# Gated linear attention and two MLPs on one core: three weight buffers, later-placed loads, and first-chunk f, k, q loaded in 768-byte rows

## The chip, the cores and the metric

The kernel runs on one core of a Trainium2 chip. The core has five engines with queues of their own: TensorE (PE in the profile; its weight loads are shown apart as PEld), VectorE (DVE), ScalarE (ACT), GpSimd (POOL) and SyncE (SP), which here issues the DMAs. Each engine takes its instructions strictly in the order of its queue and waits at the head of it for what the instruction needs. The metric is the device time of one execution in microseconds; lower is better, and the median of three runs counts.

## What is computed

Four batches, eight heads, 768 tokens and head size 48. A gated linear attention walks over the tokens of each head, and its output (3072 tokens of 384 numbers) passes through two MLPs.

```python
# q, k, v, f_logit: (4, 8, 768, 48); w_in: (384, 2048), w_out: (2048, 384)
f = 1.0 / (1.0 + np.exp(-f_logit))
state = np.zeros((B, H, D, D))
for t in range(S):
    state = f[:, :, t, :, None] * state + np.einsum('bhd,bhe->bhde', k[:, :, t], v[:, :, t])
    y[:, :, t] = np.einsum('bhd,bhde->bhe', q[:, :, t], state)
...
h = x @ w_in                                        # first MLP
x = (np.maximum(h, 0) + alpha * np.minimum(h, 0)) @ w_out
h = x @ w2_in                                       # second MLP
out = (h - np.tanh(h)) @ w2_out
```

The weights come as 64-bit floats and are turned into pairs of 32-bit parts (a rounded part and its remainder) on the chip; a product of the MLPs is made of three matmuls of such parts.

## The kernel before

**Attention.** The tokens are cut into 6 chunks of 128. A step i is one batch of one chunk (i = 4 * chunk + batch), so there are 24 steps. A step has seven stages. Stage f turns f so that channels lie on partitions (`turned`, four transposes on PE), takes exp and adds one on ACT into the one `gate` tile, and makes the running product `up` and the backward one `down` with two scans on DVE, the second of which reads `gate` too. Stage k turns k and q and multiplies them by `up` and `down` on DVE (kd, qd). Stage s0 makes the scores on PE, which ACT copies to `a` and POOL masks in the first two chunks; s1 turns kd back for the state. Stage y0 multiplies qd by the state of earlier chunks (`blocks`), y1 the masked scores by v, and the sum is split on ACT and DVE into the two parts of x. Stage m renews the state on DVE and copies it into `blocks` on ACT. From the second chunk on, some rows of x have to move to other partitions (`x_spread`, six DMAs of 32 KB for each pair of steps).

**MLPs.** A slot is one 128-wide piece of the 2048 hidden columns for one chunk's 512 tokens: nine matmuls into h, the nonlinearity and a split into gh and gl on ACT and DVE, and two slots later nine matmuls into the accumulators. The first eight pieces of chunk 0 come first (slots 0 to 7), then all sixteen of chunk 1, which need all four steps 4 to 7.

**Weights.** Each MLP's weights are 16 halves of 768 KB. `load_w` brings a half into a staging tile `raw` (pool `stg`), and `convert` decodes it: |high word| on ACT (mag), then four integer operations on DVE (L50, L52, L55, L58), a rounding copy on ACT and a subtraction on DVE (L200). `stg` has two buffers, and the load of half n+2 stands right behind the decode of half n.

**What sets the order.** The first four steps follow the hand-written list `PROLOGUE`; everything later has a due time in slots, put into `work` and sorted; Tile's scheduler then lays the instructions of that program out on each engine's queue. All DMAs go through SP's queue, at most eight under way at once: a further one waits for the completion of the one eight places ahead. The f, k and q tiles (three of each) are zero-padded from 48 to 64 columns by POOL, only in the padding (L120).

Of the kernel before, what the change touches and what calls it, by code (L numbers as in the profile page):

```python
# [25 lines left out]
SEG = C + 1  # L26
NV = 3
X3W = 2
LAG = 2
# [34 lines left out]
def tile_main(tc, q, k, v, f_logit, w1_in, w1_out, alpha, w2_in, w2_out, out, flag):  # L64
    nc = tc.nc
    with ExitStack() as ctx:
# [4 lines left out]
        stg = ctx.enter_context(tc.tile_pool(name="stg", bufs=2))  # L71
# [29 lines left out]
        for b in range(B):  # L101
            state.append(const.tile([128, NP, D], F32, name=f"state{b}"))
            t = const.tile([128, NP, 2, HW], F32, name=f"blocks{b}")
            nc.gpsimd.memset(t, 0.0)
            blocks.append(t)
# [10 lines left out]
        for nm, idle in (("f", 30.0), ("k", 0.0), ("q", 0.0)):  # L116
# [18 lines left out]
        def load_step(i):  # L135
            c, b = divmod(i, B)
            t0 = c * C
            s = {}
            for nm, a in (("f", f_logit), ("k", k), ("q", q), ("v", v)):
                if nm == "v" and c == 0:  # L140
                    s["v"], s["v3"] = first_v[b % NV]
                    nc.sync.dma_start(out=s["v"][:, :, 0:D], in_=v[b, 0:6, t0:t0 + C, :].rearrange("h t d -> t h d"))
                    for h in range(2):
                        nc.sync.dma_start(
                            out=s["v3"][:, h, :, D:64], in_=v[b, 6 + h, t0:t0 + C, :].rearrange("t (r d) -> t r d", r=3)
                        )
                    continue
                if nm == "v":
                    t = s[nm] = ld.tile([128, H, D], F32, tag=nm, name=nm, bufs=NV)
                else:  # L150
                    s[nm] = padded[nm][i % NV]
                    t = s[nm][:, :, 0:D]
                nc.sync.dma_start(out=t, in_=a[b, :, t0:t0 + C, :].rearrange("h t d -> t h d"))  # L153
            steps[i] = s

# [53 lines left out]
        def turned(a, palloc, name):  # L209

            t = palloc([128, NP, C], name)
            for p in range(NP):
                nc.tensor.transpose(t[:, p], a[:, 2 * p:2 * p + 2, :].rearrange("t h d -> t (h d)"), ident)  # L213
            return t

        def attn_f(i, palloc):
            s = steps[i]
            gv = spread(gate[:, 0:NP * SEG])
            ft = turned(s["f"], palloc, "ft")
            nc.scalar.activation(out=gv, in_=ft, func=ACTF.Exp, scale=-1.0)  # L220
# [21 lines left out]
        def attn_k(i, palloc):  # L242
            s = steps[i]
            kt, qt = turned(s["k"], palloc, "kt"), turned(s["q"], palloc, "qt")
            kd = at.tile([128, NP, C], F32, tag="kd", name="kd")
            nc.vector.tensor_tensor(out=kd, in0=kt, in1=spread(s["up"]), op=ALU.mult)
            qd = at.tile([128, NP, C], F32, tag="qd", name="qd")
            nc.vector.tensor_tensor(out=qd, in0=qt, in1=spread(s["down"][:, 1:NP * SEG + 1]), op=ALU.mult)
            s.update(kd=kd, qd=qd, a=at.tile([128, 2, NP, C], F32, tag="a", name="a"))

        def attn_s(i, half, palloc):
            s = steps[i]
            if half:
# [6 lines left out]
                return  # L260

# [20 lines left out]
        def attn_y(i, half, palloc):  # L282
            c, b = divmod(i, B)
            s = steps[i]
            if half == 0:
                y = s["y"] = palloc([128, NP, C], "y")
                if c:
                    for p in range(NP):
                        nc.tensor.matmul(  # L289
                            out=y[:, p], lhsT=blocks[b][:, p].rearrange("p h d -> p (h d)"), rhs=s["qd"][:, p],  # L290
# [47 lines left out]
        def attn_m(i, palloc):  # L338
# [18 lines left out]
            for h in range(2):  # L357
                r = slice(HW * h, HW * h + HW)
                nc.scalar.copy(out=blocks[b][r, :, h, 0:D], in_=st[r])
# [131 lines left out]
        def stage(st, i, palloc=narrow):  # L491
# [22 lines left out]
        load_step(0)  # L514
        nc.sync.dma_start(out=alpha_raw, in_=alpha.rearrange("(c p) -> c p", p=128))
        load_step(1)
        load_w(0, *halves[0])
        load_step(2)
        load_w(0, *halves[1])

        for ev in PROLOGUE:
            if ev[0] == "c":
                convert(0, ev[1])
            elif ev[0] == "l":
                load_step(ev[1])
            else:
# [11 lines left out]
        for i in range(B, NC * B):  # L538
# [6 lines left out]
            for st, t in order:  # L545
                put(t0 + t, stage, st, i)
        first = sum(ev[0] == "c" for ev in PROLOGUE)
        for n in range(first, 2 * NG):
            put((n - first) * 1.0 if n < NG else 7.5 + 1.5 * (n - NG), convert, 0, n)
# [4 lines left out]
        for n in range(2):  # L554
            put(last + 1.5, load_w, 1, *halves[n])
        for n, (g, half) in enumerate(halves):
            put(max(last + 6 + 1.5 * n, last + 2 * g + 2 * half + 2.2), convert, 1, n)
# [170 lines left out]
```

## Time and profile before

| what | us |
| --- | --- |
| median of 3 runs (1006.9 to 1009.63) | 1008.5 |
| the profiled execution | 1006.54 |
| its span, first to last instruction | 1004.7 |
| PE busy in the span | 967.0 (96%) |
| DVE busy | 553.0 (55%) |
| ACT busy | 417.4 (42%) |

PE is busy without a break from about 160 us on. All that PE lacks lies ahead of that, in the first four steps and the four steps of the second chunk, and a few microseconds at the very end. In this stretch the shares of the whole span say little, and one looks at windows and at what ended each wait.

### The profile page before, as it was taken

What the parts mean: (1) busy time and instruction counts of PE and PEld (TensorE: products, weight loads), DVE (VectorE), ACT (ScalarE), POOL (GpSimd) and SP (SyncE); (2) the same over time, 40 slices, a digit from 0 to 9 for tenths busy, and PEclk for the clock granted to TensorE, in tenths of its full rate; (3) what the DMA queues carried; (4) which work ended last, traced back from release to release, by engine and by line L of the source; (5) the groups of instructions that cost most, each with busy time, mean ns of one, the idle gap of its engine ahead of it and who ended that gap; (6) DMA issues with size and microseconds to landing.
All of it is one profiled execution on the core that took longest, in us unless ns stands there. A gap on an engine that the chain in (4) does not pass through costs nothing.

```text
span 1004.7 us, 13518 instructions
## 1 busy us (share of the span) xinstructions
PE 967.0 (96%) x5395; PEld 816.2 (81%) x5395; DVE 553.0 (55%) x889; ACT 417.4 (42%) x739; POOL 24.0 (2%) x43
## 2 busy tenths in 40 slices
PE   6689879999999999999999999999999999999997
PEld 5567657887887888888887889999999999999996
DVE  5699875355665556366547979643343433433332
ACT  4466544444444444434345755432232332322322
POOL 3111200000000000000000000000000000000000
PEclk8799779999999999999999999999999999999999
DMA  9986771012322232121004425210010010000001
GB/s 155 198 150 127 161 155 40 0 48 56 77 54 44 40 71 56 24 46 58 1 16 150 132 96 160 85 63 1 1 63 1 29 36 1 32 1 1 32 1 34
DMA packets 125030, 62.69 MB, mean 62 GB/s; under 512 B 104336, under 2 KB 109344, under 8 KB 124960
## 3 DMA queue, kind: packets, MB, share of 16 engines
q1 hardware_dynamic: 124960, 61.76, 27.4%
q8 instruction: 44, 0.72, 0.3%
q14 instruction: 26, 0.21, 0.1%
HBM read 49.55 MB, written 10.22 MB: 59 GB/s over the span
## 4 chain that ended last, share of the span: by engine, by line
PE 87%; DVE 4%; DMA 4%; SPq 2%; ACT 1%; issue 1%; DVEq 0%; ACTq 0%
PE acc L452 38%; PE h L401 13%; PE h L402 13%; PE h L403 13%; PE sc L266 2%; DMA raw<-in_moe_w_out_dram 2%; DMA raw<-in_moe_w_in_dram 2%; PE y L313 2%; PE y L289 2%; SPq L153 1%; PE m L348 1%; PE kr L257 1%; PE ft L213 1%; PE kt L213 1%; PE qt L213 1%
## 5 line engine op out<-in xcount | busy, mean ns | idle before, releaser
L401 PE MATMUL h<-x,wih 128*128 128x512 f32 x576 | 232.5, 404 | 5.9 <-DMA x<-x 2.9
L402 PE MATMUL h<-x,wih 128*128 128x512 f32 x576 | 230.1, 400 | 1.7 <-DVE x L307 1.7
L403 PE MATMUL h<-x,wil 128*128 128x512 f32 x576 | 228.1, 396 | 0.0
L423 DVE TENSOR_TENSOR gl<-g,gh 128x512 fp32r<-128x512 f32 x192 | 132.3, 689 | 82.0 <-PE acc L452 45.9
L422 ACT CAST gh<-g 128x512 fp32r<-128x512 f32 x192 | 119.0, 620 | 120.3 <-DVE g L414 61.9
L414 DVE TENSOR_TENSOR g<-h,g 128x512 f32<-128x512 f32 x96 | 66.4, 691 | 175.1 <-ACT g L413 175.0
L409 DVE SCALAR_TENSOR_TENSOR g<-neg,alpha_neg,g 128x512 f32<-128x512 f32 x96 | 73.0, 760 | 128.1 <-ACT neg L408 128.0
L413 ACT ACTIVATE g<-h 128x512 f32<-128x512 f32 x96 | 57.5, 599 | 192.1 <-PE h L403 192.1
L401 PEld LDWEIGHTS h<-x,wih 128*128 128x128 f32 x576 | 108.9, 189 | 28.6 <-issue 3.6
L403 PEld LDWEIGHTS h<-x,wil 128*128 128x128 f32 x576 | 108.8, 189 | 26.2 <-issue 0.2
L452 PE MATMUL acc<-wol,gh 128*128 128x384 f32 x384 | 128.4, 334 | 0.0
L452 PE MATMUL acc<-woh,gh 128*128 128x384 f32 x384 | 128.3, 334 | 0.0
L452 PE MATMUL acc<-woh,gl 128*128 128x384 f32 x384 | 126.9, 334 | 0.0
L402 PEld LDWEIGHTS h<-x,wih 128*128 128x128 f32 x576 | 108.9, 189 | 21.1 <-DVE x L307 2.1
L452 PE MATMUL acc<-gl,woh 128*128 128x512 f32 x288 | 115.2, 400 | 0.0
L452 PE MATMUL acc<-gh,wol 128*128 128x512 f32 x288 | 113.1, 393 | 0.0
L452 PE MATMUL acc<-gh,woh 128*128 128x512 f32 x288 | 109.1, 401 | 0.0
L407 ACT ACTIVATE g<-h 128x512 f32<-128x512 f32 x96 | 57.3, 596 | 106.5 <-PE h L403 101.5
L452 PEld LDWEIGHTS acc<-woh,gh 128*128 128x128 f32 x384 | 72.1, 188 | 4.8
L452 PEld LDWEIGHTS acc<-wol,gh 128*128 128x128 f32 x384 | 72.1, 188 | 4.3
L452 PEld LDWEIGHTS acc<-woh,gl 128*128 128x128 f32 x384 | 72.0, 188 | 0.0
L452 PEld LDWEIGHTS acc<-gh,woh 128*128 128x128 f32 x288 | 53.9, 188 | 13.9 <-issue 0.4
(92 smaller groups left out, 975.4 us busy)
## 6 DMA issues: line engine op xcount, KB each, us to landing
raw<-in_moe_w_out_dram SPq DMA_DIRECT2D x16, 768.0 KB, 4.6
raw<-in_moe_w_in_dram SPq DMA_DIRECT2D x8, 768.0 KB, 4.6
f<-in_f_logit_dram SPq DMA_DIRECT2D x24, 192.0 KB, 4.4
k<-in_k_dram SPq DMA_DIRECT2D x24, 192.0 KB, 3.9
q<-in_q_dram SPq DMA_DIRECT2D x24, 192.0 KB, 3.9
raw<-in_moe_w_in_dram SPq DMA_DIRECT2D x16, 288.0 KB, 5.1
x1d<-o SPq DMA_DIRECT2D x6, 768.0 KB, 4.3
x1raw<-x1d SPq DMA_DIRECT2D x6, 768.0 KB, 5.0
```

The costliest lines, as they stand in the source:

```text
L213: nc.tensor.transpose(t[:, p], a[:, 2 * p:2 * p + 2, :].rearrange("t h d -> t (h d)"), ident)
L266: nc.tensor.matmul(out=sc[h][:, p], lhsT=s["kd"][r, p], rhs=s["qd"][r, p], start=True, stop=True)
L401: nc.tensor.matmul(out=h, lhsT=a, rhs=xh[:, r], start=(r == 0), stop=False)
L402: nc.tensor.matmul(out=h, lhsT=a, rhs=xl[:, r], start=False, stop=False)
L403: nc.tensor.matmul(out=h, lhsT=b, rhs=xh[:, r], start=False, stop=(r == 2))
L407: nc.scalar.activation(out=g, in_=h, func=ACTF.Relu)
L409: nc.vector.scalar_tensor_tensor(out=g, in0=neg, scalar=alpha_neg[:, fc:fc + 1], in1=g, op0=ALU.mult, op1=ALU.add)
L413: nc.scalar.activation(out=g, in_=h, func=ACTF.Tanh)
L414: nc.vector.tensor_tensor(out=g, in0=h, in1=g, op=ALU.subtract)
L422: nc.scalar.copy(out=gh, in_=g)
L423: nc.vector.tensor_tensor(out=gl, in0=g, in1=gh.bitcast(F32), op=ALU.subtract)
L452: nc.tensor.matmul(out=t, lhsT=a, rhs=b, start=first and i == 0, stop=final and i == 2)
```

## The change

- `stg` gets a third buffer (`NR`), and `blocks` has two tiles instead of four; the copies into `blocks` move from stage m to stage s0 of the step that needs them.
- Loads have events and due times of their own. A weight load of half n+3 comes 1.2 slots behind the conversion of half n, a step's loads behind the last stage that uses their buffers; the v loads of the first chunk are apart from the f, k, q loads (`load_v`). `PROLOGUE` is rewritten, with ("f", 4) in it.
- For the first four steps (`EARLY`) f, k and q are read in rows of four tokens, 768 bytes, into a partition per (head pair, four tokens), as two DMAs of 96 KB for each tile; the second half of step 0's tiles is issued from ACT. They are turned by eight ordinary matmuls with the identity as moving operand rather than by four transposes. What comes out has the tokens in another order in PSUM, and the reading operation on ACT or DVE puts them right (`like`).
- POOL sets the whole f, k and q tiles (L126), 512 columns each, ahead of these loads.

```diff
+EARLY = B
+PAD = 4 * D + 16
+NR = 3
 PROLOGUE = (
...
+    ("l", 0), ("a", 0), ("l", 1), ("v", 0), ("l", 2), ("v", 1), ("w", 0), ("v", 2),
...
-        stg = ctx.enter_context(tc.tile_pool(name="stg", bufs=2))
+        stg = ctx.enter_context(tc.tile_pool(name="stg", bufs=NR))
...
-                t = const.tile([128, H, HW], F32, name=f"{nm}{j}")
-                nc.gpsimd.memset(t[:, :, D:HW], idle)
+                t = const.tile([128, H * HW], F32, name=f"{nm}{j}")
+                nc.gpsimd.memset(t, 30.0 if nm == "f" else 0.0)
...
+                    t = padded[nm][i % NV]
+                    if i < EARLY:
+                        s[nm] = t[:, 0:2 * PAD].rearrange("p (h x) -> p h x", h=2)
+                        for h in range(2):
+                            (nc.scalar if i == 0 and h else nc.sync).dma_start(
+                                out=s[nm][:, h, 0:4 * D],
+                                in_=a[b, h::2, t0:t0 + C, :].rearrange("p (t j) d -> p t (j d)", j=4),
+                            )
+                        continue
...
+        def turned(i, nm, palloc):
+            a = steps[i][nm]
+            if i >= EARLY:
...
+            t = palloc([128, 4, 128], nm + "t")
+            for j in range(4):
+                for h in range(2):
+                    nc.tensor.matmul(
+                        out=t[HW * h:HW * h + HW, j], lhsT=a[:, h, j * D:j * D + HW], rhs=ident, start=True, stop=True
+                    )
+            return t.rearrange("p j (h t) -> p h t j", h=NP)
+        def like(i, a):
+            return a.rearrange("p h (t j) -> p h t j", j=4) if i < EARLY else a
...
+            if c:
+                for h in range(2):
+                    r = slice(HW * h, HW * h + D)
+                    nc.scalar.copy(out=blocks[i % 2][r, :, h, 0:D], in_=state[b][r])
...
-                if i + NV < NC * B and not B <= i + NV < B + NV:
-                    load_step(i + NV)
...
-            if n + 2 < len(halves):
-                load_w(m, *halves[n + 2])
...
+            if i >= B + NV:
+                put(t0 - NV * (1.85 if c < 3 else 3) + 0.8, load_step, i)
...
+            if n + NR < 2 * NG:
+                put(max(t, -0.2) + 1.2, load, 0, n + NR)
```

How this moves the queues, at the places that matter below:

SP's queue at the very start, before (f0 is the first f buffer, step 0; va and vb are the two v tiles of a step; raw is a weight half):

```order
L153 DMA f0_130<-in_f_logit_dram 128x8x48
L153 DMA k0_136<-in_k_dram 128x8x48
L153 DMA q0_142<-in_q_dram 128x8x48
L142 DMA va0_148<-in_v_dram 128x6x48
L144 DMA vb0_149<-in_v_dram 128x3x16 x2
L515 DMA alpha_raw_129<-in_moe_alpha_dram 16x128
L153 DMA f1_132<-in_f_logit_dram 128x8x48
L153 DMA k1_138<-in_k_dram 128x8x48
L153 DMA q1_144<-in_q_dram 128x8x48
L142 DMA va1_152<-in_v_dram 128x6x48
L144 DMA vb1_153<-in_v_dram 128x3x16 x2
L172 DMA raw_174<-in_moe_w_in_dram 48x3x512
```

And in the changed kernel:

```order
L562 DMA alpha_raw_125<-in_moe_alpha_dram 16x128
L172 DMA va0_144<-in_v_dram 128x6x48
L174 DMA vb0_145<-in_v_dram 128x3x16 x2
L156 DMA f0_126<-in_f_logit_dram 128x1x192
L156 DMA f1_128<-in_f_logit_dram 128x1x192
L156 DMA k0_132<-in_k_dram 128x1x192
L156 DMA q0_138<-in_q_dram 128x1x192
L156 DMA f1_128<-in_f_logit_dram 128x1x192
L156 DMA k1_134<-in_k_dram 128x1x192 x2
L156 DMA q1_140<-in_q_dram 128x1x192 x2
L156 DMA f2_130<-in_f_logit_dram 128x1x192 x2
L156 DMA k2_136<-in_k_dram 128x1x192 x2
```

The first f load stood first and now stands fifth, the f, k, q loads of steps 0 to 2 stand together, and the first weight half (raw_174 before) comes ten issues later, behind q2 and the second step's v.

ACT's queue at the start of the changed kernel, which before began with the table load:

```order
L156 DMA f0_126<-in_f_logit_dram 128x1x192
L156 DMA k0_132<-in_k_dram 128x1x192
L156 DMA q0_138<-in_q_dram 128x1x192
L255 ACT_TABLE_LOAD
L255 ACTIVATE gate_106<-ft_190 128x4x128
```

Three DMA issues stand ahead of the table load and of the first exp.

SP's queue around the third weight half (raw_315 before, w_out), with the loads of steps 3 and 4 ahead of it:

```order
L153 DMA f0_130<-in_f_logit_dram 128x8x48
L153 DMA k0_136<-in_k_dram 128x8x48
L153 DMA q0_142<-in_q_dram 128x8x48
L153 DMA f1_132<-in_f_logit_dram 128x8x48
L153 DMA k1_138<-in_k_dram 128x8x48
L142 DMA va0_148<-in_v_dram 128x6x48
L144 DMA vb0_149<-in_v_dram 128x3x16 x2
L164 DMA raw_315<-in_moe_w_out_dram 128x2x768
L153 DMA q1_144<-in_q_dram 128x8x48
```

And the same half (raw_262) in the changed kernel, where f1 and k1 are those of step 4:

```order
L194 DMA raw_257<-in_moe_w_in_dram 48x3x512
L198 DMA raw_257<-in_moe_w_in_dram 16x3x512
L194 DMA raw_257<-in_moe_w_in_dram 48x3x512
L198 DMA raw_257<-in_moe_w_in_dram 16x3x512
L186 DMA raw_262<-in_moe_w_out_dram 128x2x768
L172 DMA va0_144<-in_v_dram 128x6x48
L174 DMA vb0_145<-in_v_dram 128x3x16 x2
L164 DMA f1_128<-in_f_logit_dram 128x8x48
L164 DMA k1_134<-in_k_dram 128x8x48
```

It now stands directly behind the second half, ahead of step 4's loads, and waits for no decode.

DVE's queue just ahead of the end of chunk 1's attention, before; x1_123 is the second part of chunk 1's x, and dec, mag, wil and wol belong to weight halves:

```order
L55 SCALAR_TENSOR_TENSOR dec_1392<-raw_1279,dec_1392 128x768
L354 TENSOR_TENSOR state2_116<-u_1039,inv_763 128x192
L200 TENSOR_TENSOR wil_1338<-dec_1333,wih_1337 128x768
L58 SCALAR_TENSOR_TENSOR dec_1392<-raw_1279,dec_1392 128x768
L353 TENSOR_TENSOR u_1171<-m_1162,state3_119 128x192
L354 TENSOR_TENSOR state3_119<-u_1171,inv_931 128x192
L200 TENSOR_TENSOR wol_1397<-dec_1392,woh_1396 128x768
L224 TENSOR_SCALAR gate_106<-gate_106 128x4x128
L323 TENSOR_TENSOR x3_1025<-y_1126,x3_1025 128x128
L226 SCALAR_TENSOR_TENSOR up_1725<-gate_106,reset_103 128x516
L323 TENSOR_TENSOR x1_123<-y_1126,x1_123 128x3x128
```

And in the changed kernel, where x1_119 is that tile:

```order
L57 TENSOR_SCALAR dec_1540<-mag_1537 128x768
L60 SCALAR_TENSOR_TENSOR dec_1540<-raw_1407,dec_1540 128x768
L222 TENSOR_TENSOR wil_1489<-dec_1484,wih_1488 128x768
L63 SCALAR_TENSOR_TENSOR dec_1540<-raw_1407,dec_1540 128x768
L55 TENSOR_SCALAR mag_1589<-mag_1589 128x768
L365 TENSOR_TENSOR x3_1070<-y_1166,x3_1070 128x128
L395 TENSOR_TENSOR u_1216<-m_1207,state3_113 128x192
L259 TENSOR_SCALAR gate_106<-gate_106 128x4x128
L57 TENSOR_SCALAR dec_1592<-mag_1589 128x768
L222 TENSOR_TENSOR wol_1545<-dec_1540,woh_1544 128x768
L396 TENSOR_TENSOR state3_113<-u_1216,inv_976 128x192
L365 TENSOR_TENSOR x1_119<-y_1166,x1_119 128x3x128
```

Two more halves are wholly decoded ahead of the last x than before: 14 subtractions into wil and wol stand ahead of it from the start, where 12 stood.

## Rows read from the trace of the kernel before

**Rows 1.** Page: span; busy tenths of PE and DVE in 40 slices.

```profile
span 1004.7 us, 13518 instructions
...
PE   6689879999999999999999999999999999999997
...
DVE  5699875355665556366547979643343433433332
```

**Rows 2.** Windows: length, then each engine's busy us (instructions), PE clock, DMA share, GB/s.

```profile
6.63:54.85 48.22, 33.48 (x295) 27.18 (x295) 34.68 (x60) 21.46 (x39) 6.79 (x8) 0.79 1.21 183
54.85:124.70 69.85, 65.51 (x430) 53.13 (x430) 62.93 (x103) 42.62 (x78) 11.71 (x8) 0.93 0.72 144
124.70:132.90 8.20, 2.62 (x21) 2.03 (x21) 6.22 (x12) 1.86 (x3) 0.00 (x0) 0.70 0.91 203
132.90:160.00 27.10, 25.43 (x130) 19.28 (x130) 23.13 (x38) 14.09 (x25) 0.00 (x0) 0.90 0.59 126
```

**Rows 3.** Waits of DVE, 6 to 55 us: total us, times, longest.

```profile
DVE up L226 <- ACT gate L222: 7.6, 5, 4.0
DVE mag L50 <- ACT mag L49: 7.3, 2, 4.7
```

**Rows 4.** Waits of DVE, 55 to 133 us.

```profile
DVE mag L50 <- ACT mag L49: 6.7, 5, 2.5
```

**Rows 5.** Timeline of the first 20 us: start, us, what, [idle before <- releaser].

```profile
0.82 0.44 SPq L153 DMA_DIRECT2D f<-in_f_logit_dram  x1
...
2.11 1.28 ACT L220 ACT_TABLE_LOAD   x1 [2.11 <-DVE gate L96]
...
2.35 0.52 POOL L104 MEMSET blocks<- 128x512 f32 x1
...
5.25 0.60 ACT L220 ACTIVATE gate<-ft 128x512 f32<-128x512 f32 x1 [1.85 <-PE ft L213]
...
6.63 1.23 DVE L226 TENSOR_TENSOR_SCAN up<-gate,reset 128x516 f32<-128x516 f32 x1 [4.03 <-ACT gate L222]
...
18.61 0.56 DVE L50 TENSOR_SCALAR mag<-mag 128x768 f32<-128x768 f32 x1 [2.56 <-ACT mag L49]
```

**Rows 6.** DMA in 0 to 60 us: queue, packets, MB, share of 16 engines.

```profile
q1 hardware_dynamic: 36336, 10.04, 113.1%
```

**Rows 7.** DMA rate in 40 slices of 775 to 830 us, around one x1 load.

```profile
GB/s 0 0 0 0 0 0 0 0 0 0 0 0 6 0 0 12 0 0 0 159 368 46 7 171 366 27 0 0 0 0 0 0 0 0 12 0 0 0 0 0
```

**Rows 8.** Timeline: f turned on PE, and y products of 64 columns.

```profile
22.98 0.66 PE L213 MATMUL ft<-ident,f 128*128 128x128 f32 x4
...
49.58 0.88 PE L301 MATMUL y<-a,va 128*64 128x128 f32 x12
```

**Rows 9.** DVE groups by line, 55 to 125 us: busy us, mean ns | idle before.

```profile
L58 DVE SCALAR_TENSOR_TENSOR dec<-raw,dec 128x768 int32<-128x768 int32 x9 | 9.0, 997 | 0.0
L55 DVE SCALAR_TENSOR_TENSOR dec<-raw,dec 128x768 int32<-128x768 int32 x9 | 8.5, 948 | 0.0
...
L52 DVE TENSOR_SCALAR dec<-mag 128x768 int32<-128x768 int32 x9 | 4.9, 547 | 0.0
...
L200 DVE TENSOR_TENSOR wol<-dec,woh 128x768 fp32r<-128x768 f32 x5 | 4.7, 945 | 0.0
L50 DVE TENSOR_SCALAR mag<-mag 128x768 f32<-128x768 f32 x8 | 4.4, 554 | 4.9 <-ACT mag L49 4.9
...
L246 DVE TENSOR_TENSOR kd<-kt,up 128x512 f32<-128x512 f32 x4 | 2.7, 682 | 0.0
```

**Rows 10.** Weight loads (tile raw), 12 to 160 us: issue to landing.

```profile
DMA to landing us min/median/max: 3.7/5.4/9.2
```

**Rows 11.** Tile x, 90 to 140 us: DMA issue ns min/median/max; then timeline rows.

```profile
L336 SPq DMA_DIRECT2D x<-x x12: 586/592/3642, 95.5 to 132.6; - x12
```

**Rows 12.** Timeline from 126 to 145 us: chunk 1's first h, and the break behind it.

```profile
132.88 0.77 PE L401 MATMUL h<-x,wih 128*128 128x512 f32 x1 [2.86 <-DMA x<-x]
...
141.56 0.91 ACT L49 ACTIVATE mag<-raw 128x768 f32<-128x768 f32 x1 [7.39 <-DMA raw<-in_moe_w_in_dram]
...
144.22 0.50 PE L401 MATMUL h<-x,wih 128*128 128x512 f32 x1 [1.67 <-ACT neg L408]
```

More of the change, by code (lines that the diff above doesn't have):

```diff
@@ L102, in tile_main @@
             state.append(const.tile([128, NP, D], F32, name=f"state{b}"))
+        for b in range(2):
             t = const.tile([128, NP, 2, HW], F32, name=f"blocks{b}")
@@ L115, in tile_main @@
         padded = {}
-        for nm, idle in (("f", 30.0), ("k", 0.0), ("q", 0.0)):
+        for nm in ("f", "k", "q"):
             padded[nm] = []
             for j in range(NV):
-                t = const.tile([128, H, HW], F32, name=f"{nm}{j}")
-                nc.gpsimd.memset(t[:, :, D:HW], idle)
+                t = const.tile([128, H * HW], F32, name=f"{nm}{j}")
+                nc.gpsimd.memset(t, 30.0 if nm == "f" else 0.0)
                 padded[nm].append(t)
@@ L140, in load_step @@
                 if nm == "v" and c == 0:
[L141 to L146, printed above, removed]
                     continue
@@ L154, in load_step, with load_v @@
             steps[i] = s
+        def load_v(i):
+            b = i
+            s = steps[i]
+            s["v"], s["v3"] = first_v[b % NV]
+            nc.sync.dma_start(out=s["v"][:, :, 0:D], in_=v[b, 0:6, 0:C, :].rearrange("h t d -> t h d"))
+            for h in range(2):
+                nc.sync.dma_start(
+                    out=s["v3"][:, h, :, D:64], in_=v[b, 6 + h, 0:C, :].rearrange("t (r d) -> t r d", r=3)
+                )
         raws = {}
@@ L260, in attn_s @@
                 return
+            c, b = divmod(i, B)
+            if c:
+                for h in range(2):
+                    r = slice(HW * h, HW * h + D)
+                    nc.scalar.copy(out=blocks[i % 2][r, :, h, 0:D], in_=state[b][r])
             sc = [palloc([128, NP, C], f"sc{h}") for h in range(2)]
@@ L510, in convert, with load @@
             convert_b(m, *halves[n])
-            if n + 2 < len(halves):
-                load_w(m, *halves[n + 2])
[L514 to L519, printed above, removed]
+        def load(m, n):
+            load_w(m, *halves[n])
         for ev in PROLOGUE:
@@ L523, in tile_main @@
                 convert(0, ev[1])
+            elif ev[0] == "w":
+                load(0, ev[1])
             elif ev[0] == "l":
                 load_step(ev[1])
+            elif ev[0] == "v":
+                load_v(ev[1])
+            elif ev[0] == "a":
+                nc.sync.dma_start(out=alpha_raw, in_=alpha.rearrange("(c p) -> c p", p=128))
             else:
@@ L545, in tile_main @@
             for st, t in order:
-                put(t0 + t, stage, st, i)
+                if ("f", i) not in PROLOGUE or st != "f":
+                    put(t0 + t, stage, st, i)
+            if i >= B + NV:
+                put(t0 - NV * (1.85 if c < 3 else 3) + 0.8, load_step, i)
         first = sum(ev[0] == "c" for ev in PROLOGUE)
-        for n in range(first, 2 * NG):
-            put((n - first) * 1.0 if n < NG else 7.5 + 1.5 * (n - NG), convert, 0, n)
+        for n in range(2 * NG):
+            t = (n - first) * 1.0 if n < NG else 7.5 + 1.5 * (n - NG)
+            if n >= first:
+                put(t, convert, 0, n)
+            if n + NR < 2 * NG:
+                put(max(t, -0.2) + 1.2, load, 0, n + NR)
         put(3 * HALF + HALF - 3, load_part, 4 * HALF - 1)
@@ L553, in tile_main @@
         put(last + 1.5, check_decay)
-        for n in range(2):
-            put(last + 1.5, load_w, 1, *halves[n])
+        for n in range(NR):
+            put(last + 1.5, load, 1, n)
         for n, (g, half) in enumerate(halves):
-            put(max(last + 6 + 1.5 * n, last + 2 * g + 2 * half + 2.2), convert, 1, n)
+            t = max(last + 6 + 1.5 * n, last + 2 * g + 2 * half + 2.2)
+            put(t, convert, 1, n)
+            if n + NR < 2 * NG:
+                put(t + 1.2, load, 1, n + NR)
         for c in range(1, NC):
```

29 lines of the change are left out of this document (14 added, 15 removed), and 7 rows, old and new, of the table PROLOGUE.

## Prediction

> **What bounds the kernel now.** I read the busy slices of the page first: from the seventh slice on PE is busy in nine tenths or more of every slice but the last [rows 1], so nothing that the change does after about 160 us can show in the time, and the whole question is when PE gets its last gap. Then I cut the beginning into windows at the points that the work itself gives: 6.63 us, DVE's first scan; 54.85, the first chunk's x is complete; 124.70, the second chunk's x is complete on DVE; 132.88, the first matmul on that x [rows 2, 12]. In the first window DVE is busy for 34.7 of 48.2 us and PE for 33.5; in the second DVE for 62.9 of 69.9 and PE for 65.5, part of it at a lowered clock [rows 2]. DVE has a chain that cannot be reordered (scan, scan, products, one step after the other) and the weight decodes besides, so it sets both points: idle 13.5 us in the first window and 6.9 in the second, 20.4 together. The waits of DVE name the cause of 14.0 of these: it waits for mag, ACT's first step of a decode, 7.3 and 6.7 us [rows 3, 4], and ACT in turn for the weight load. Waits of the up scan for the gate make 7.6 [rows 3], 4.0 of which is the one ahead of 6.63 us [rows 5], so 3.6 inside. The remaining 2.8 are single waits for casts and products. So the loads are late and the engine behind them is DVE, although PE is the busier one.
>
> **The start.** POOL now sets a whole 512-column tile ahead of each load. Such a set takes 0.52 us [rows 5]; q's first tile is the seventh of them in POOL's order, which reaches the tiles at about 2.4 us, so it is done at about 2.4 + 7 x 0.52 = 6.0, and 6.2 with the small operation between them. ACT's third load waits for that, and behind it stand the table load and the first exp. With 0.44 us for an issue (as f's on SP) and 1.28 for the table load [rows 5], exp can start at 6.2 + 0.5 + 1.3 = 8.0 instead of 5.25, and the first scan comes 1.38 later as before: 9.4 instead of 6.63 [rows 5], a loss of 2.8 us. It is not hidden, since DVE has nothing else then. Before, the table load ended at 3.39 with ACT idle until 5.25 [rows 5].
>
> The Trainium skill (ScalarE: Activation LUTs, What ACT_TABLE_LOAD costs) adds about 1.38 us of drain to the 1.28 us of such a load. No run here shows it, as ACT had nothing to do behind the load; by it the first scan would come at 10.8 and the time below would be 1.4 us longer.
>
> **First-chunk loads.** The first 60 us moved 36336 packets, nearly all of 192 bytes, in 113% of 16 engines' time [rows 6]: 1.13 x 16 x 60 us / 36336 = 30 ns each. A tile of f, k or q was 1024 packets, 1.9 us of all engines; now it is 256 packets of 768 bytes. These cost between 30 ns (by packet) and 120 ns (by byte, as the short ones); at the 368 GB/s of a load in long rows [rows 7] 33 ns, and I take that, since it is the rate of the same engines on long rows: 0.5 us a tile, 1.4 less, 17 us over twelve tiles. It is no gain by itself; it is what lets the three weight halves and the next steps arrive. Twice as many issues cost SP 12 x 0.44 = 5 us more of its queue.
>
> **Turning.** Eight matmuls with 64 columns replace four transposes. Six matmuls of that shape, which the profile counts as twelve, took 0.88 us at full clock, so eight take 1.2, against 0.66 [rows 8]: 0.5 us more, 1.1 at half clock, for twelve tiles, 6 to 13 us of PE. PE has 14.7 us idle in the first window [rows 2] and DVE turns to kd, qd or a decode meanwhile, so I cost it at nothing; without that cover it would be 0.5 to 1 us for each of four steps' f, 2 to 4. The strided reading of PSUM that puts the tokens right is in no row: between nothing and a doubling of the eight products of 0.68 us [rows 9], 5.5 us; I take nothing, because the number of elements is the same.
>
> **Weight loads with three buffers.** A load takes 5.4 us in the median from issue to landing, up to 9.2 [rows 10]. Before, it was issued when the decode one half earlier had freed its buffer, so one decode (0.55 + 0.55 + 0.95 + 1.0 + 0.95 = 4.0 us [rows 9]) was all that surely covered it. Now two decodes and the attention work between them stand ahead of its use: 8 us or more. Most of the 14.0 us should go. The very first half goes the other way: it is issued ten places later, 4.4 us, while DVE reaches it only 2.8 + 1.3 = 4.1 us later (the late start, and one scan more ahead of it). DVE's wait there was 2.56 us [rows 5]; it stays at about 2.9. I leave 3.0 for all mag waits. The third half is issued behind the second and has no wait.
>
> **The order on DVE.** Up to chunk 1's last x the new queue has, beside the same attention and MLP work, three more of each first and second decode step, two more of each of the other three (0.55, 0.55, 0.95, 1.0 and 0.95 us [rows 9]), and one scan of 1.23 less [rows 5]: 1.65 + 1.65 + 1.9 + 2.0 + 1.9 - 1.2 = 7.9 us more. That work is only moved ahead, but it stands ahead of the point that PE waits for, so it counts fully there. Moving the state copies on ACT from m to s0 costs nothing: ACT is busy 42.6 of 69.9 us [rows 2], the copies are as many, and the state they need is a chunk old.
>
> **The end of the stretch.** From chunk 1's x to its first matmul it took 132.9 - 124.7 = 8.2 us [rows 2, 12]. One of the six small loads of x was held for 3.6 us instead of 0.59 [rows 11], behind a weight half just issued. Now the last half is issued ahead of those, but three loads that wait for PE's turning of k and q (2 x 0.66 [rows 8]) stand before them: 8.2 - 3.0 + 1.3 = 6.5. Behind that, PE stops once more for 1.67 us, for ACT, which had waited 7.39 us for a weight half [rows 12]; with all halves issued by then, this goes.
>
> **The sum.** Chunk 1's x is complete at 9.4 + (34.7 + 62.9) + 7.9 = 114.9 plus DVE's idle time. (The same sum for the kernel before: 6.6 + 97.6 + 20.4 = 124.6.) For the idle time: mag 3.0; gate waits 1.0, as f is there early and the products cover exp; the other 2.8 as before; 1.2 for the first nonlinearity, which DVE now reaches before slot 0's matmuls are done. Together 8.0. So x at 122.9, the first matmul at 129.4 instead of 132.9, 3.5 us earlier, and 1.7 behind it: 5.2 us. PE's work from there on is the same. Against the profiled execution, 1006.5 - 5.2 = 1001.3; that execution lies 2.0 below the median of 1008.5, so for the median 1003.3.
>
> **The rivals.** In all of them the free number is the idle time of DVE, I, and the gain is 13.2 - I: at I = 13.2 nothing is left.
> - *The decodes ahead of x eat it.* DVE's 7.9 us of added work and the 2.8 us of start are certain, the vanished waits are not; casts on ACT may come late when two decodes are in flight. With I = 11 to 13 the gain is 0 to 2 us: 1007.5. For it: PE is itself busy for 65.5 of 69.9 us in the second window [rows 2], so DVE may wait for its products. Against it: DVE waited there almost only for mag [rows 4].
> - *The loads stay late, and the kernel gets slower.* The queue has eight places; twelve loads of short rows for steps 4 to 6 stand ahead of the fourth half, and its issue waits behind those that wait for PE. If only the second window's mag waits go, or if 768 bytes cost 120 ns, the first window keeps its 13.5 and I = 17: 3.8 us slower, 1012.3. If nothing goes, I = 20.4 and it is 7.2 slower, 1015.7. It decides from I = 13.2 on: more than half of the 14.0 us must vanish. For it: DMA has no room in the first 60 us [rows 6]. Against: the second and third halves are issued ahead of those loads.
> - *The table load holds ACT for longer than its row.* If ACT is held once more for the 1.28 us of it [rows 5], the first scan is at 10.7 and the time 1004.6. The rows speak neither for nor against, since ACT was idle behind the load before; I hold it for one in five, inside the forecast.
> - *The waits go altogether*, the first half's too, and I = 4: 9.2 us gained, 999.3.
>
> **How the numbers follow.** I give the forecast 0.50 (with 0.10 of it for the longer table load; 1000 to 1006 in it), the eaten gain 0.25, the late loads 0.20, the complete gain 0.05. The forecast's time stands: 1003.3. The range takes in the complete gain with a microsecond below it and the milder late loads: 998 to 1012. About 0.3%, or 3 us, is what a measurement of this kernel can tell from no change; the forecast lies 5 us off, so a tenth of its chance falls under 3 us. Faster by over 0.3%: 0.45 + 0.05 = 0.50. Same: 0.25 with 0.05, and 0.02 of the late loads: 0.32. Slower: 0.18.
>
> **What would show it.** In the changed profile: the first scan at 9.4 us; DVE's mag waits at 3 us or less up to chunk 1's x, with the largest at the first half; the first chunk's x at about 46 us (9.4, then the first window's 34.7 of work without the 2.9 of step 4's operations that the new queue puts behind that x, and some 4.4 idle); the second's at 123; the first matmul on it at 129 to 130, and no stop of PE behind it. If the two x come at 46 and 123, but PE's end doesn't follow, the sum after the first matmul is wrong, the lowered clock first of all. If mag waits are gone and the second x is still not before 125, the order of DVE has eaten the gain. If mag waits stand at 10 us or more, the loads are the cause.

## The result

The changed kernel takes 1017.65 us in the median (1016.37 to 1018.54), the kernel before on the same chip 1007.7. The ratio is 1.0095, 95% interval 1.0075 to 1.0116: slower by about 1%, where 0.5% faster was forecast, and outside the range of 998 to 1012. The profiled execution took 1018.54 us with a span of 1016.7 (before: 1006.54 and 1004.7).

The page of after, busy tenths in 40 slices, is to be held against [rows 1]:

```profile
span 1016.7 us, 13824 instructions
...
PE 966.4 (95%) x5539; PEld 817.0 (80%) x5539; DVE 552.0 (54%) x889; ACT 418.3 (41%) x739; POOL 28.5 (3%) x41
...
PE   5599659999999999999999999999999999999996
...
DMA  3898570024233222112014425110010010000001
```

As before, PE is full from the seventh slice on, but for the last; nearly all that differs lies ahead of about 160 us. The same cut as in [rows 2] (first scan, chunk 0's x complete, chunk 1's x complete), columns: stretch, its length, then busy time of PE, PEld, DVE, ACT and POOL, granted clock, DMA share, GB/s:

```profile
12.03:62.22 50.19, 37.07 (x428) 31.49 (x426) 31.63 (x55) 19.55 (x34) 6.79 (x8) 0.86 0.81 147
62.22:143.87 81.65, 65.19 (x432) 51.28 (x431) 73.06 (x119) 48.45 (x85) 14.28 (x8) 0.87 0.83 178
```

DVE's work up to chunk 1's x is 31.6 + 73.1 = 104.7 us, its idle time 18.6 + 8.6 = 27.2; before it was 97.6 and 20.4. The start is later too. These rows of the timeline (start, duration, engine, line) lead to the first scan, as [rows 5] did before:

```profile
2.90 1.15 ACTq L156 DMA_DIRECT2D f<-in_f_logit_dram  x1
...
6.57 1.28 ACT L255 ACT_TABLE_LOAD   x1 [6.57 <-POOL q L126]
...
8.62 2.37 PE L242 MATMUL ft<-ident,f 128*64 128x128 f32 x18 [8.62 <-DMA f<-in_f_logit_dram]
...
10.64 0.60 ACT L255 ACTIVATE gate<-ft 128x512 f32<-128x512 f32 x1 [2.79 <-PE ft L242]
...
12.03 1.23 DVE L261 TENSOR_TENSOR_SCAN up<-gate,reset 128x516 f32<-128x516 f32 x1 [9.42 <-ACT gate L257]
```

The settings on POOL and the table load came as forecast (ACT free at 7.85), but the first load of f, issued at 2.9, was not used before 8.62: 5.7 us for a load of 96 KB, with others like it under way. The DMA view of 12 to 20 us, when only such loads were under way, shows why:

```profile
DMA  2222222222222222222222222222222222222222
GB/s 92 92 92 92 92 96 88 96 88 88 92 92 84 92 92 92 96 88 92 84 92 88 81 92 92 92 88 96 92 88 96 77 92 92 84 92 92 92 92 92
DMA packets 977, 0.73 MB, mean 91 GB/s; under 512 B 32, under 2 KB 977, under 8 KB 977
...
q1 hardware_dynamic: 883, 0.66, 24.9%
q10 hardware_dynamic: 94, 0.07, 2.6%
```

All 40 slices stand at two tenths of 16 engines and about 92 GB/s. A packet took 0.275 x 16 x 8 us / 977 = 36 ns, what the prediction took (33); but the time of only about four engines was ever in use. The packet records of the trace say the same: in this stretch never fewer than four and never more than seven packets are under way, and in 65% of the time exactly four. The 24 first-chunk loads are 2.36 MB, 25.6 us at 92 GB/s. A tile of 256 packets over 4 engines takes 256 x 36 ns / 4 = 2.3 us, more than the 1.9 of 1024 short packets over 16. And all that SP issues behind them came late; the timeline of SP and ACT:

```profile
10.33 3.65 SPq L156 DMA_DIRECT2D q<-in_q_dram  x2
...
24.14 0.70 SPq L194 DMA_DIRECT2D raw<-in_moe_w_in_dram  x1
...
28.18 3.13 SPq L156 DMA_DIRECT2D f<-in_f_logit_dram  x2
...
32.10 0.89 ACT L54 ACTIVATE mag<-raw 128x768 f32<-128x768 f32 x1 [5.87 <-DMA raw<-in_moe_w_in_dram]
```

At 10.33 us the two issues of q take 3.65 us, and the first weight half is issued at 24.14 (before: 10.16). It was not the limit of eight loads under way that held the first of these two: by the trace's landing records the load eight places ahead had landed at 9.55. The issues themselves took longer. DVE's waits, in the first and in the second window (before [rows 3, 4]; columns: total, times, longest):

```profile
DVE up L261 <- ACT gate L257: 11.8, 2, 9.4
DVE mag L55 <- ACT mag L54: 9.6, 2, 5.3
DVE kd L281 <- PE kr L294: 4.3, 2, 2.9
...
DVE mag L55 <- ACT mag L54: 5.3, 3, 4.7
```

The waits for weight halves are 14.9 us, not fewer than before. The 14.0 that the prediction reads from [rows 3, 4] go up to 133 us; up to chunk 1's x, at 124.69, the second part was 4.9 and not 6.7, so 12.2 us compare with the 14.9:

```profile
DVE mag L50 <- ACT mag L49: 4.9, 4, 2.5
```

The end of the stretch did get shorter, 3.1 us instead of 8.2 [rows 12]; timeline of DVE, SP and PE:

```profile
143.32 0.55 DVE L365 TENSOR_TENSOR x<-y,x 128x384 fp32r<-128x384 f32 x1
...
143.90 3.79 SPq L378 DMA_DIRECT2D x<-x  x6
...
147.00 0.76 PE L440 MATMUL h<-x,wih 128*128 128x512 f32 x1 [4.36 <-DMA x<-x]
```

### The profile page after: what moved, and what is told of

It reads as the page before. It is cut to its first block, busy times and chain, and to the rows that moved or that the text cites. A ratio compares the mean times of both kernels' runs of the same rounds, so it can differ in the third digit from the quotient of the medians.

```text
span 1016.7 us, 13824 instructions
## 1 busy us (share of the span) xinstructions
PE 966.4 (95%) x5539; PEld 817.0 (80%) x5539; DVE 552.0 (54%) x889; ACT 418.3 (41%) x739; POOL 28.5 (3%) x41
## 4 chain that ended last, share of the span: by engine, by line
PE 91%; DMA 2%; SPq 2%; DVE 2%; POOL 1%; ACT 1%; issue 1%; DVEq 0%; ACTq 0%; POOLq 0%
PE acc L491 39%; PE h L440 14%; PE h L441 13%; PE h L442 13%; PE sc L308 2%; PE y L355 2%; PE y L331 2%; DMA raw<-in_moe_w_in_dram 2%; SPq L156 1%; PE kt L237 1%; PE m L390 1%; PE qt L237 1%; PE kr L294 1%; PE ft L237 1%; POOL a L314 1%; DMA k<-in_k_dram 1%
## 5 line engine op out<-in xcount | busy, mean ns | idle before, releaser
L491 PE MATMUL acc<-wol,gh 128*128 128x384 f32 x384 | 128.4, 334 | 0.0
L491 PEld LDWEIGHTS acc<-gh,woh 128*128 128x128 f32 x288 | 53.9, 188 | 13.7 <-issue 0.2
```

What stands on the lines that cost most here:

```text
L491: nc.tensor.matmul(out=t, lhsT=a, rhs=b, start=first and i == 0, stop=final and i == 2)
```

## The experiments

Three theories: A, the first-chunk loads are served by 4 of 16 engines, because the outermost dimension of their pattern is the 4 heads; B, the new order (more decodes ahead of chunk 1's x, other places of the loads); C, the turning by products. All ratios are against the kernel before on the same chip.

### Rows and order, apart

**e1_spread32**: the 32 groups of tokens go outside, the heads inside; the turned tile is read accordingly.

```
-  in_=a[b, h::2, t0:t0 + C, :].rearrange("p (t j) d -> p t (j d)", j=4),
+  in_=a[b, h::2, t0:t0 + C, :].rearrange("p (t j) d -> t p (j d)", j=4),
-  return t.rearrange("p j (h t) -> p h t j", h=NP)
+  return t.rearrange("p j (t h) -> p h t j", h=NP)
```

> The changed kernel with one thing different: each first-chunk load walks its source with the 32 groups of tokens outside and the 4 heads inside, where the changed kernel has the 4 heads outside. Same packets of 768 bytes, same number of loads, same order. Theory A (a load whose outermost dimension is 4 is served by 4 of the 16 DMA engines, so that each load takes about four times as long and the eight places in flight hold SP's queue): f of step 0 lands 2 us after its issue instead of 5.5, the DMA share in 10 to 20 us rises from 0.27 to 0.8 or more, the first weight half is issued at 11 to 14 us instead of 24, chunk 0's x is complete near 48 us, chunk 1's near 125, first matmul on it near 132, time 1001 to 1006. Theory B (the new order, 14 decodes ahead of x, is the cost): the loads get quicker but x of chunk 1 stays behind 135 and the time at or above 1012. Theory C (the turning and the strided reads are the cost): no change from 1017.7.

Measured: 1005.3 us, ratio 0.9981 (0.9967 to 0.9994). The same two windows as above, in e1 (the profiled execution, 1003.3, is the shortest of its ten):

```profile
9.45:48.12 38.67, 29.83 (x418) 25.83 (x414) 32.26 (x55) 19.47 (x34) 7.72 (x8) 0.96 1.02 177
48.12:130.28 82.16, 66.05 (x432) 51.89 (x431) 73.00 (x119) 48.29 (x85) 14.30 (x8) 0.89 0.86 180
```

Its DMA view of 9 to 13 us, where too only loads of f, k and q were issued:

```profile
DMA packets 889, 0.61 MB, mean 151 GB/s; under 512 B 101, under 2 KB 889, under 8 KB 889
...
q1 hardware_dynamic: 889, 0.61, 58.2%
```

Its timeline, with ACT's first exp, the first scan, SP's issues of f and k, the first weight half and the first matmul on chunk 1's x:

```profile
6.63 1.28 ACT L255 ACT_TABLE_LOAD   x1 [6.63 <-POOL q L126]
8.06 0.60 ACT L255 ACTIVATE gate<-ft 128x512 f32<-128x512 f32 x1 [0.15 <-PE ft L242]
...
9.45 1.23 DVE L261 TENSOR_TENSOR_SCAN up<-gate,reset 128x516 f32<-128x516 f32 x1 [6.84 <-ACT gate L257]
...
9.76 1.25 SPq L156 DMA_DIRECT2D f<-in_f_logit_dram  x2
11.05 1.25 SPq L156 DMA_DIRECT2D k<-in_k_dram  x2
...
15.91 0.61 SPq L194 DMA_DIRECT2D raw<-in_moe_w_in_dram  x1
...
133.33 0.77 PE L440 MATMUL h<-x,wih 128*128 128x512 f32 x1 [4.75 <-DMA x<-x]
```

One swapped pair of dimensions gives back 12.3 us by the medians, 11.5 by the two ratios (the runs are from different chips). Theory A holds. The landing records of the two traces count the engines: the f load that SP issues at about 3.1 us raises its semaphore by four landings in the changed kernel (7.81 to 8.49 us, with a single early update at 4.27) and by sixteen in e1 (5.40 to 5.91). C falls: e1 turns by the same products, and the strided operations take what they took before (exp 0.60 us, the products 0.68). But x of chunk 1 is at 130.3, not near 125: part of B is there too. The DMA share (0.58, not 0.8 or more) and the first weight half (15.9 us, not by 14) miss as well. The rows of SP say why, though no run tests it: they hold four issues, one in 0.645 us, and 96 KB in that time are 152 GB/s, against 151 measured. So a tile of two loads takes 1.3 us of SP's queue even on all engines. The Trainium skill (DMA: Bandwidth & Descriptors, "Why a DMA increments its semaphore by 16 and not by 1") says that a DMA runs on the largest number of engines, up to 16, that divides the slowest dimension of both its patterns: 4 for 4 heads onto 128 partitions, 16 for 32 groups. The two traces agree, with DMA shares of 0.275 and 0.58.

**e2_short_rows** (the changed kernel with `EARLY = 0`: rows of 192 bytes and transposes again), **e3_before_rows4** and **e4_before_rows32** (the kernel before with the new rows, the turning and POOL's whole-tile settings alone, the second with e1's two lines):

```
-EARLY = B
+EARLY = 0
```

> The changed kernel with the first chunk's f, k and q again in rows of 192 bytes and turned by transposes, as in the kernel before; three buffers, the new order, the placement of the loads and the full-tile settings stay. Theory A (rows on 4 engines): the loss goes, and what the rest is worth is seen: 1002 to 1009. Theory B (the order): the loss stays, 1012 to 1018. Theory C (turning): as theory A, so this run separates B alone from the others.

> The kernel before with only the new rows: first-chunk f, k, q in rows of 768 bytes with the 4 heads outside, turned by products; two buffers and the old order stay. Theory A: slower, 1012 to 1020, with a DMA share near 0.3 in the first 20 us. Theory B (the order is the cost): no change or faster, 1000 to 1009. Theory C (turning): slower, as theory A, but with a DMA share as before.

> The kernel before with only the new rows, but with the 32 groups of tokens outside. Theory A: 1000 to 1007, as short rows no longer fill the DMA engines, and the difference to the run with 4 outside is 8 us or more. Theory C: as slow as the run with 4 outside.

With e1 they make a full table (median us, ratio):

| rows | old order, two buffers | new order, three buffers |
|---|---|---|
| 192 bytes | 1007.0 | 1007.3, 1.0004 (0.9992 to 1.0016) |
| 768 bytes, heads outside | 1010.2, 1.0029 (1.0014 to 1.0044) | 1017.65, 1.0095 |
| 768 bytes, tokens outside | 1001.6, 0.9941 (0.9918 to 0.9964) | 1005.3, 0.9981 |

Heads outside cost 8.6 us in the old order (e3 stays below the 1012 to 1020 expected) and 12.3 in the new one. Rows of 768 bytes over all engines gain 5.4 in the old order. The new order with its buffers never gains: 0.3, 7.5 (6.6 by the ratios) and 3.7 us slower, the first within what can be told from nothing. (The row of 192 bytes has POOL's whole-tile settings in the new order alone: its first scan is at 9.43 us, 6.63 before.)

### What the third buffer does

**e5_new_two_buffers** is e1 with two buffers; **e6_before_three_buffers** is e4 with three; **e6a_before_copies_moved** is e4 with the state copies at s0 in two tiles, which e6 needs for space, and two buffers.

```
e5: -NR = 3
    +NR = 2
    -... ("w", 1), ("w", 2), ("s0", 0) ... ("c", 0), ("l", 4)
    +... ("w", 1), ("s0", 0) ... ("c", 0), ("w", 2), ("l", 4)
e6: -stg = ... tc.tile_pool(name="stg", bufs=2)
    +stg = ... tc.tile_pool(name="stg", bufs=3)
    -load_w(m, *halves[n + 2])
    +load_w(m, *halves[n + 3])
```

> The changed kernel with the loads spread (32 groups of tokens outside) and with two weight buffers instead of three; the third half is issued behind the first decode, every later load behind the last use of its buffer. In DVE's order 11 casts' remainders (wil, wol) stand ahead of chunk 1's last x instead of 14. Theory D (the third buffer lets more decodes stand ahead of chunk 1's x, where each costs its 4 us of DVE): faster than with three, 997 to 1003, x of chunk 1 at 118 to 124 us. Theory E (the third buffer does save waits for weight halves, and the rest of the new order is the cost): slower than with three, 1006 to 1010, with waits of DVE for mag of 14 us or more up to that x.

> The kernel before with the spread rows of 768 bytes and a third weight buffer (the state copies moved to two tiles and to s0, as in the changed kernel, to make room; loads three halves ahead). 14 remainders stand ahead of chunk 1's last x where the two-buffer form has 11. Theory D: slower than the two-buffer form (1001.6), 1004 to 1008. Theory E: faster, 995 to 1000.

> As the run before with three buffers, but with two: only the state copies go to two tiles and to s0. DVE's order has 14 remainders ahead of chunk 1's last x here too. If the number of decodes ahead of x is what costs, 1004 to 1008, as with three buffers; if the third buffer by itself costs (its waits or its loads in SP's queue), 1000 to 1003, as the form with the old copies.

Measured: e5 1001.35, 0.9957 (0.9939 to 0.9975); e6 1006.1, 0.9996 (0.9983 to 1.0009); e6a 1011.9, 1.0057 (1.0038 to 1.0077). Both windows of e4, for comparison:

```profile
10.88:50.30 39.42, 31.06 (x417) 26.09 (x413) 32.29 (x56) 20.59 (x38) 7.77 (x8) 0.96 1.00 175
50.30:123.94 73.64, 64.00 (x430) 50.86 (x430) 64.59 (x107) 42.26 (x78) 8.55 (x8) 0.95 0.83 156
```

The second window of e5:

```profile
48.99:123.93 74.94, 65.11 (x432) 51.79 (x431) 61.94 (x103) 42.77 (x78) 8.77 (x8) 0.93 0.80 160
```

Both windows of e6:

```profile
9.79:59.55 49.76, 36.41 (x419) 30.90 (x415) 39.14 (x66) 23.04 (x38) 6.66 (x8) 0.83 1.07 199
59.55:130.93 71.38, 62.44 (x430) 50.18 (x430) 68.91 (x110) 46.83 (x82) 8.99 (x8) 0.94 0.80 167
```

Both windows of e6a:

```profile
9.78:55.31 45.53, 35.46 (x420) 30.17 (x416) 34.98 (x59) 20.50 (x35) 6.20 (x8) 0.85 0.98 187
55.31:137.39 82.08, 66.13 (x430) 52.60 (x430) 71.31 (x115) 45.82 (x82) 7.79 (x8) 0.87 0.73 148
```

DVE's wait for weight halves in e6's second window:

```profile
DVE mag L52 <- ACT mag L51: 1.5, 3, 0.6
```

In e6 the third buffer does what it is for: the waits of the second window fall to 1.5 us (6.2 in e4). But up to chunk 1's x DVE now works 39.1 + 68.9 = 108.0 us, 11.2 more than in e4 (96.9), for the decodes that the buffer lets go ahead. x comes at 130.9 instead of 123.9. e5 is the reverse of e1: 11 decodes instead of 14, 94.0 us of work instead of 105.3, x at 123.9 instead of 130.3. In time this is 4.0 us by the medians, but only 2.4 by the ratios, whose intervals overlap a little. e6a has 14 decodes ahead with two buffers: DVE then works 106.3 us and still waits 12.4 for mag. At 1011.9 it is slower than either reading of it expected, and 5.8 us slower than e6, which has as many decodes ahead and the third buffer. So the buffer by itself saves time, and what it lets go ahead of x costs more than that: theory D, as far as e4 against e6 shows it. It is not the whole account: e13 below has three buffers and 105.8 us of work ahead of x, and is as fast as e5.

### The path by which the loads cost

**e12_changed_weights_on_pool** is the changed kernel with all weight halves issued by POOL; **e13_spread_weights_on_pool** and **e14_two_buffers_weights_on_pool** are e1 and e5 with the same edit.

```
 in load_w: -nc.sync.dma_start(
            +nc.gpsimd.dma_start(
```

> The changed kernel (heads outside, 1017.7) with the weight halves issued by POOL instead of SP, so that they no longer stand behind the first-chunk loads and the step loads in SP's order. Theory A1 (the first-chunk loads cost by what stands behind them on SP: weight halves 14 us late): the first half is issued at 8 to 10 us instead of 24, DVE's waits for mag in the first window fall from 9.6 to 4 or less, time 1008 to 1012; f, k, q of step 3 stay late. Theory A2 (they cost by their own landing: f, k and q themselves come late, waits for ft and kt): no more than 2 us gained, 1015 to 1018.

> The changed kernel with spread rows (1005.3) and the weight halves issued by POOL. Theory F (in SP's order weight halves and step loads hold each other, and that is why three buffers don't take the waits for mag away): mag waits up to chunk 1's x fall from 9.2 to 4 or less, x of chunk 1 at 122 to 126, time 998 to 1002. Theory G (the halves are late for another reason: DVE frees a buffer late, or the DMA engines are full): mag waits stay at 8 or more, 1004 to 1008. Rival H: POOL's masks now stand behind loads that wait for DVE, PE waits for the masks: 1006 to 1012.

> The form with spread rows and two weight buffers (1001.35), weight halves issued by POOL. Theory F: mag waits from 10.5 to 6 or less, time 996 to 1000. Theory G: 1000 to 1003. Rival H: 1003 to 1010.

Measured: e12 1018.2, 1.0129 (1.0088 to 1.0170); e13 1001.4, 0.9944 (0.9924 to 0.9964); e14 1003.0, 0.9962 (0.9946 to 0.9978). In e12 the first weight half is issued 16 us earlier, and nothing is gained. Its timeline of POOL and SP:

```profile
8.00 0.72 POOL L194 DMA_DIRECT2D raw<-in_moe_w_in_dram  x1
...
12.65 11.70 SPq L156 DMA_DIRECT2D q<-in_q_dram  x2
```

DVE's waits in e12 up to chunk 0's x:

```profile
DVE up L261 <- ACT gate L257: 9.4, 1, 9.4
DVE qd L283 <- PE qt L242: 8.2, 2, 6.7
DVE mag L55 <- ACT mag L54: 6.8, 3, 4.3
```

With the halves there DVE waits for q, 8.2 us instead of 0.8 in the changed kernel, and chunk 0's x comes at 72.4 us instead of 62.2. So taking the halves out of SP's order does not help, and A1 as expected fails. But A2 is not shown alone: the halves now run beside f, k and q and slow them. The two issues of q take 11.70 us instead of 3.65, and in 12 to 20 us a packet of 768 bytes takes 72 ns instead of 37 (means of the packet records). How the loss divides between f, k and q themselves and what stands behind them stays open. In e13 the queue of its own takes the second window's mag waits from 6.2 to 2.8 us, as theory F has it, but the first window's rise from 3.0 to 6.6, since DVE's order there now begins six halves instead of three. The sum does not fall (9.4, theory G's side), the whole idle time does (15.6 to 11.2 us), and the time falls in F's range. With two buffers (e14) nothing is gained. Theory F is right for the second window alone.

### The start, and the end of the stretch

**e7_before_rows32_blocks_late** (e4, the four state blocks set on POOL behind the tiles of f, k, q), **e8_two_buffers_split_spread** and **e11_three_buffers_split_spread** (e5 and e1; half of the last six small loads of x issued by ACT), **e9_two_weight_four_step_buffers** (e5 with four tiles each for f, k, q, v), **e10_both** (e9 with e8's edit).

```
e8:  -nc.sync.dma_start(out=x[r0:r0 + 16, :, r, o] ...
     +(nc.scalar if c == 1 and b == B - 1 and h else nc.sync).dma_start(out=x[r0:r0 + 16, :, r, o] ...
e9:  -for j in range(NV): ... padded[nm][i % NV] ... bufs=NV
     +for j in range(NV + 1): ... padded[nm][i % (NV + 1)] ... bufs=NV + 1
```

> The kernel before with the spread rows of 768 bytes, and POOL sets the four state blocks behind the tiles of f, k and q instead of ahead: the settings of f end 2.1 us earlier. If the first scan sets the start, it comes at 8.8 instead of 10.9 us; 10 remainders stand ahead of chunk 1's last x instead of 11. 997 to 1001. If the start is hidden by what follows (the weight half, the table load), no change from 1001.6.

> The form with spread rows, the new order and two weight buffers (1001.35), with one thing different: of the six small loads that spread chunk 1's last x, three are issued by ACT instead of SP. There PE waited 6.6 us for them, as SP stood behind a load of k. If that wait is on the path, it falls to 3 to 4 us, the first matmul on chunk 1's x comes at 127 instead of 129.6, and the time is 998 to 999.5. Rival: ACT's casts behind the three issues come later and the gain is given back within the next 30 us: 1001 to 1002.

> The same form (1001.35) with four buffers for each of f, k, q and v instead of three; the places of the loads in the program stay. Theory F (weight halves come late because SP stands, in order, at loads of k, q and v that wait for PE): SP's waits for PE up to chunk 1's x (21 us in the form with three) fall below 10, DVE's waits for mag from 10.5 to 6 or less, x of chunk 1 at 118 to 121, time 997 to 1000. Theory G (two weight buffers by themselves set these waits, since a load can only start when a decode has ended): mag waits stay at 9 or more, time 1001 to 1003.

> The four step buffers and the split spread together, on the form with two weight buffers. If both act on the path, the gains add: 994 to 998. If the second one only moves a stop, as the better of the two alone.

> The changed kernel with spread rows (three weight buffers, 1005.3), with the last spread of x split between SP and ACT as above. PE waited 4.7 us for it there; three issues fewer in a row are 1.9 us. If the end of the stretch passes to the time one to one, as forecast: 1003.0 to 1004.0. If it doesn't: 1005 to 1006.

Measured: e7 1004.3, 0.9976 (0.9962 to 0.9990); e8 1002.4, 0.9942 (0.9925 to 0.9960); e9 1000.5, 0.9930 (0.9906 to 0.9953); e10 1001.2, 0.9929 (0.9909 to 0.9949); e11 1005.9, 0.9977 (0.9964 to 0.9990).

e7 misses: the first scan came at 8.55 as expected, 2.3 us earlier than in e4, and the kernel is slower than e4, not faster (the intervals just overlap). Its second window has 17.5 us of idle DVE instead of 9.0, most of it waits for mag (7.2), the nonlinearity (5.1), the gate (2.1) and casts (2.4), after an order that has moved. Two microseconds at the start are not passed on. The split of the small loads misses too, in e8, e10 (994 to 998 expected) and e11: the intervals overlap those of the forms without it. In e8 the stretch from x to the first matmul got shorter, 4.0 instead of 5.6 us, but x itself came 3.4 us later than in e5. In e11 the issuing ended 2.2 us behind x instead of 3.8, and the stretch got longer, 3.8 instead of 3.1. The last issue is not what the first matmul waits for: in e1 it starts at 133.33, while the sixth issue ends at 134.10. Timeline of e8, ACT's issues and the first matmul:

```profile
127.35 2.19 ACTq L378 DMA_DIRECT2D x<-x  x3
...
131.28 0.77 PE L440 MATMUL h<-x,wih 128*128 128x512 f32 x1 [4.48 <-DMA x<-x]
```

e9 brings x of chunk 1 to 120.2 as expected, 3.8 us earlier than e5, but neither through the mag waits (9.9 us, theory G's side) nor through SP's, which still stands about 30 us for PE from the start to x (27 in e5); and the first matmul on it gains only 1.2 (128.4). Its interval overlaps e5's. Its median is the lowest of all, 0.7% below the kernel before; e4, e5, e8, e9, e10 and e13 can't be told apart.

## Why the prediction was wrong

**The step that failed** is "0.5 us a tile", in the paragraph on the first-chunk loads, which shares a tile among all 16 engines. Price per packet and number of packets were right (36 against 33 ns, 256); the number of engines was not: 4, so 2.3 us a tile. I had taken 16 from the loads of before, which have the 128 tokens outside. The diff has the pattern with `p`, the 4 heads, outermost; the prediction makes nothing of it. It is worth 12.3 us (e1, 11.5 by the ratios), the whole loss of 10. On all engines the step would still have been too low: with 0.645 us for an issue where 0.44 was priced, SP needs 1.3 us for the two loads of a tile (e1).

**The ledger**, against the profiled execution (1018.5, forecast 1001.3, 17.2 apart): first scan 12.0 instead of 9.4, 2.6; DVE's work 104.7 instead of 105.5, -0.8; its idle time 27.2 instead of 8.0, 19.2; end of the stretch 3.1 instead of 6.5, -3.4; behind it 0.4 better. The sum is 17.2. Of the 19.2 us of idle time, 11.6 go with the swapped dimensions of e1 (27.2 to 15.6); the other 7.6 belong to the mag waits and the rest below.

- *Start*: the path over POOL, ACT's third issue and the table load is right. Without the slow f (e1) the first scan is at 9.45, forecast 9.4. The longer hold of ACT that one rival supposes is not to be seen in e1: the table load ends at 7.91, and exp starts at 8.06.
- *Loads*: the "late loads" rival had the direction, with I = 20.4 at worst and a chance of 0.20; I was 27.2. The reason given there (120 ns a packet) was wrong, and its milder case is added up wrongly: 13.5 us of the first window and 6.9 - 6.7 of the second are 13.7, not 17.
- *Turning*: nothing, right. e4 gains although it turns by products, and the strided reads cost nothing.
- *Mag waits*: 3.0 us forecast, 14.9 measured, and 9.2 with spread rows. With 14 decodes ahead this step was wrong by itself; 7.6 us of idle time are left in e1 over the forecast. Its start was misread too: 12.2 us were to be had up to chunk 1's x, not 14.0, so the other waits were 4.6 and not 2.8, and the sum should have had 9.8 us idle, a gain of 3.4. A buffer more removed waits where it was alone (e6, second window: 1.5), not in the new order (e1).
- *DVE's order*: 7.9 us more work forecast, 7.1 measured (e1: 7.7). Right in size, and it is what makes the third buffer a loss: from e4 to e6 DVE's work grows by 11.2 us and its idle time falls by 3.1.
- *End of the stretch*: better than forecast, 3.1 us; the small loads were issued at once, at 143.90 behind an x complete at 143.87.
- *"PE's work from there on is the same"*: right for the stop that goes, and a little too simple. PE's 30 us behind the first matmul on chunk 1's x, first in the kernel before:

```profile
132.88:162.88 30.00, 28.33 (x142) 21.63 (x143) 24.08 (x39) 14.73 (x26) 0.00 (x0) 0.91 0.54 115
```

In e1, with 14 decodes ahead of that x:

```profile
133.33:163.33 30.00, 30.00 (x142) 24.34 (x143) 19.78 (x31) 14.73 (x27) 0.00 (x0) 0.95 0.05 11
```

In e4, with 11:

```profile
126.77:156.77 30.00, 26.54 (x135) 19.99 (x136) 21.13 (x35) 12.90 (x22) 0.00 (x0) 0.88 0.65 129
```

PE stands 1.7 us with 12 decodes done, not at all with 14, 3.5 us with 11 in the old order. Decodes put ahead of x give part of their price back here: in e1 the first matmul is 0.45 us later than before and the profiled execution 3.25 us shorter. The stop explains 1.7 of these 3.7. The granted clock, 0.91 in these 30 us before and 0.95 in e1, is worth 30 x 0.04 = 1.2 us more, by estimate; what the last 0.8 are is open. Over all runs the time behind that matmul is no constant: it is 864.5 us in e6a (14 decodes ahead, granted clock 0.98 in the 30 us) and 874.5 in e7 (10 decodes, 0.83). So x alone does not give the time.

Open too: why DVE idles 17.5 us in e7, and why a buffer more for f, k, q and v (e9) leaves SP's waits for PE where they were.

## What to carry to other kernels

Longer rows make a load cheaper only if it still reaches all DMA engines: look at the outermost dimension of both patterns, and put one that 16 divides there (by the rule cited with e1; 4 and 32 were tried here). In this trace a constant two tenths of DMA share, with issues that take longer, was the sign. A further buffer changes what the consumer does first, not only when data are there: count the work that it lets go ahead of the point that others wait for.

## What was unexpected of the hardware

- A load with 4 heads outside ran at 92 GB/s and a DMA share of 0.275 over 16 engines; the same bytes in the same packets with 32 outside at 151 GB/s and 0.58, where SP issued one load in 0.645 us.
- Weight halves on a queue of their own (e12) ran beside the loads with 4 heads outside, and a packet of 768 bytes then took 72 ns instead of 37.
- POOL's masks of one size took between 0.63 and 5.96 us in the changed kernel (median 1.19); in e5 none took more than 1.68. The long ones fell into a stretch in which DVE had hardly a gap; the cause was not tried.
- Six small issues spread over two queues (e11) ended 1.6 us sooner behind x, and the first matmul on that x came 0.8 us later.
